# Attention and two gated MLPs on one core: the third stage of batch 1 placed before the first stage of batch 2

## The chip, the cores and the metric

The program runs on one core of a Trainium2 chip. The metric is device time in microseconds (us) of one execution. The core has a matrix engine (TensorE, PE in the profile), two elementwise engines (VectorE, DVE, and ScalarE, ACT), a general engine (GpSimd, POOL), and DMA engines that are fed by queues; nearly all transfers here are issued by SyncE (SP), some by POOL. Every engine works through its own list in order and waits on semaphores for the others.

## The reference

`q`, `k`, `v` have 4 batches, 12 heads, 448 rows and 64 columns, all float32. First attention, then two MLPs on the 1792 rows that it leaves:

```
q_n, k_n = rmsnorm(q, g_q), rmsnorm(k, g_k)
attn = softmax(q_n @ k_n.T / 8)            # per batch and head, 448 x 448
x = (attn @ v), heads side by side          # 1792 x 768
x = ((x @ w_a) * (x @ w_b)) @ w_out         # 768 -> 1536 -> 768
h = x @ w_in                                # 768 -> 2048
g = max(h, 0) + alpha * min(h, 0)
out = g @ w_out2                            # 2048 -> 768
```

## The kernel before

Products are made in float16 with a high and a low half of each number: a product of two tiles is three matmuls (high by high, high by low, low by high; `prod`). The kernel works batch by batch (448 rows), and the MLPs of a batch are four stages: **a** (`x @ w_a`, `x @ w_b` and their product, 24 units of 18 matmuls), **y** (times `w_out`, 12 units of 18), **h** (times `w_in`, then the activation, 16 units of 18) and **o** (times the last weight, 24 units of 12, then a transposition and the store). `a1` is stage a of batch 1, the second batch. The line `stages` lists the order. The stages `o2`, `y3` and `o3` use a product scheme with seven instead of eight block products; the weight sums for it are made by small steps in a list called `back`.

Attention runs ahead of the MLPs, in between their units. `att_steps` walks over 84 score tiles of two 128-row blocks each (21 for each batch). For one tile it issues the scores on PE (`scores`, 8 matmuls, tile `s`), the softmax on DVE and ACT (`soft`: L421 maximum, L434, L438 exponentials), the division and the split in halves (`probs`: L483 on ACT, L484 on DVE, tiles `p16`), DMA transposes into `pT`, and every three and a half tiles the product with v (`pv`, 24 matmuls into the one PSUM buffer `x`) and its split into the two halves of an `X` chunk (`pv_out`: L534 on ACT, L535 on DVE). Six chunks of 128 columns make the input of stage a of the next batch. `RATE` says how many of these tiles are issued during a stage, spread evenly over its units; before stage a of a batch, what is missing is issued at once.

Stage a ends with a scale that needs all 12 products: the product tiles are `ab32` (L1080 on DVE), ACT sums their squares (L1083), PE adds over the partitions (`tot`, into the same PSUM buffer as `pv`), DVE sums the columns (L135) and makes a power of two (`power`: L117, L120, L123), and ACT and DVE split the 12 tiles with it into halves `AB` (L894, L895). Where stage y of the same batch follows at once (`stages_after`), this is issued at once; otherwise it becomes a list of `tasks`, one for each following unit. Stage y splits each result with the same two lines into `Y` (also L894 and L895), stage h makes `G` (L1186, L1187, L1172, L1173).

Memory: `slot` has 35 buffers of 1792 bytes per partition for X, AB, Y and G. `raw` has 5 larger buffers, in which weights were converted earlier, and which the `back` steps use (one for what they load, one for sums). `BACK` says how many `back` steps are run with each unit of a stage that has no task.

The order on each engine is made from this program by a scheduler, which may move an instruction past others of its engine where nothing forbids it.

Of the kernel before, what the change touches and what calls it, by code (L numbers as in the profile page):

```python
# [9 lines left out]
F16 = mybir.dt.float16  # L10
BF16 = mybir.dt.bfloat16
I32 = mybir.dt.int32
I64 = mybir.dt.int64
# [6 lines left out]
def attention_gated_mlps_kernel(  # L20
# [16 lines left out]
    B, H, S, D = q.shape  # L37
# [11 lines left out]
    raw_p = ctx.enter_context(tc.tile_pool(name="raw", bufs=5))  # L49
# [17 lines left out]
    def slot(name):  # L67

        return slot_p.tile([128, 2, S], F16, tag="slot", name=name)
# [454 lines left out]
        d["x"] = ps  # L524

    X, Y, AB, G = {}, {}, {}, {}

    def pv_out(g):
        d = P[g]
        b, p = divmod(g, NP)  # L530
        ps = d["x"][:, 0:S]
        X[b, p] = x = slot(f"x{b}_{p}")
        s = sx[:, b:b + 1] if b == 0 else 2.0 ** -14
        nc.scalar.activation(out=x[:, 0], in_=ps, func=AF.Copy, scale=s)  # L534
        nc.vector.scalar_tensor_tensor(  # L535
            out=x[:, 1], in0=ps, scalar=s, in1=x[:, 0], op0=ALU.mult, op1=ALU.subtract
        )
        P[g] = None
# [5 lines left out]
    def att_steps():  # L544
# [3 lines left out]
        for m in range(total + 3):  # L548
# [41 lines left out]
            if done < B * NP and 2 * (m - 1) >= (done + 1) * NI:  # L590
                pv(done)
                pv_out(done)
                fin = done
                done += 1
            yield fin


    stages = "a0 y0 h0 o0 a1 y1 a2 h1 o1 y2 h2 a3 o2 y3 o2 h3 o3".split()
    FAST = ("o2", "y3", "o3")
    OPEN = "h2"  # L600
    PIECES = {"o2": [range(2), range(2, 3)]}
# [114 lines left out]
    for st in stages:  # L716
        n, parts, _ = CHAINS[st[0]]
# [536 lines left out]
            G.pop((b, f))  # L1254


    BACK = {"a2": 1, "o1": 1, "y2": 2, "a3": 3, "o2": 1, "y3": 1}
    RATE = {"a0": 4, "y0": 5, "h0": 4, "o0": 8, "a1": 14, "y1": 7, "a2": 4, "h1": 4, "o1": 8, "y2": 6}

    if True:  # L1260
        load_qk(0)
# [17 lines left out]
        n, done = 0, 0  # L1279
# [18 lines left out]
        for i, st in enumerate(stages):  # L1298
            s, b = st[0], int(st[1])
# [7 lines left out]
            if st == OPEN:  # L1307
# [9 lines left out]
                late["t"] = ctx.enter_context(tc.tile_pool(name="lt", bufs=4))  # L1317
            state["back"] = BACK.get(st, 0)
            n, parts, _ = CHAINS[s]
# [5 lines left out]
            else:  # L1325
                gen = gen[s](b)
            want, acc = 3 * RATE.get(st, 0), 0
            for _ in gen:
# [34 lines left out]
```

## Time and profile before

| | |
|---|---|
| median of 3 runs | 1214.35 us (1212.06 to 1216.56) |
| the profiled execution | 1215.08 us |
| its span, first to last instruction | 1213.0 us |
| PE busy | 1145.4 us, 94% of the span |
| DVE, ACT, POOL busy | 816.5, 770.1, 108.2 us |
| mean granted PE clock | 0.98 of full speed |
| HBM | 184 GB/s over the span |

In the rows below a stretch or a start is counted in us from the start of the span. Busy PE counts a matmul from its start to its end at whatever clock was granted, so a stretch in which PE is busy all the time can still be slow.

### The profile page before, as it was taken

How to read it: one execution, taken by the hardware profiler on the slowest of the kernel's cores; microseconds unless marked ns; L12 is line 12 of the kernel's file. 1: busy time of each engine (PE TensorE's matmuls, PEld its weight loads, DVE VectorE, ACT ScalarE, POOL GpSimd, SP SyncE). 2: the span in 40 equal slices, each digit the busy share in tenths (PEclk: the TensorE clock that was granted, in tenths of full speed). 3: DMA queues.
4: the chain of work that ended last, by engine and by line, in shares of the span. 5: the costliest groups of instructions: out<-in, count | busy, mean ns of one | idle time of the engine just before them, and what ended most of it. 6: DMA issues, size and time to landing. Idle time of an engine off the chain costs nothing. (4 is left out here: it accounts for less than half of the span.)

```text
span 1213.0 us, 20078 instructions
## 1 busy us (share of the span) xinstructions
PE 1145.4 (94%) x7144; PEld 650.6 (54%) x7144; DVE 816.5 (67%) x1695; ACT 770.1 (63%) x1543; POOL 108.2 (9%) x176
## 2 busy tenths in 40 slices
PE   6997999899989799998999999999999999999997
PEld 3553554445434344444445554544555558996597
DVE  7898999999899666677754376554356677523631
ACT  7998999999899666767534366564255335513532
POOL 1000000000001000000012100122200562000000
PEclk9997999999989899998999999999999999999999
DMA  7658999999999999987985677898834798873465
GB/s 190 174 163 211 315 326 329 288 298 305 309 246 308 252 237 253 248 199 173 198 225 152 159 175 164 199 222 190 228 117 135 247 299 284 272 210 107 129 188 171
DMA packets 319267, 269.78 MB, mean 222 GB/s; under 512 B 178464, under 2 KB 275232, under 8 KB 319168
## 3 DMA queue, kind: packets, MB, share of 16 engines
q1 hardware_dynamic: 311376, 246.41, 75.9%
q0 software_dynamic: 7792, 22.10, 6.3%
q8 instruction: 56, 0.92, 0.3%
q14 instruction: 43, 0.35, 0.1%
HBM read 179.77 MB, written 43.25 MB: 184 GB/s over the span
## 5 line engine op out<-in xcount | busy, mean ns | idle before, releaser
L110 PEld LDWEIGHTS <-w 128*128 128x128 f16 x4104 | 398.2, 99 | 393.5 <-issue 39.6
L110 PE MATMUL p<-x,w 128*128 128x448 f16 x1728 | 336.3, 354 | 0.5 <-DVE ab L1080 0.4
L110 PE MATMUL p<-y,w 128*128 128x448 f16 x1152 | 221.6, 352 | 1.4 <-DVE t L1187 1.3
L110 PEld LDWEIGHTS <-ws 128*128 128x128 f16 x1386 | 132.5, 98 | 3.3 <-DMA ws<-f_o_S 2.7
L110 PE MATMUL p<-ab,w 128*128 128x448 f16 x648 | 129.7, 359 | 1.3 <-ACT ab L894 1.2
L110 PE MATMUL p<-g,w 128*128 128x448 f16 x576 | 119.8, 362 | 4.6 <-ACT g L1172 3.5
L421 DVE TENSOR_REDUCE nm<-s 128x2 f32<-128x896 f32 x84 | 91.2, 1086 | 33.5 <-PE s L110 33.3
L483 ACT ACTIVATE p<-pf,ri 128x448 f16<-128x448 f32 x126 | 81.8, 665 | 35.9 <-DMA pT<-p 27.4
L484 DVE SCALAR_TENSOR_TENSOR p<-pf,ri,p 128x448 f16<-128x448 f32 x126 | 84.6, 680 | 28.1 <-ACT p L483 28.0
L110 PE MATMUL l<-g,ws 128*128 128x224 f16 x960 | 94.2, 259 | 1.8 <-DMA ws<-f_o_S 1.8
L438 ACT ACTIVATE pf<-s,nm,esc 128x448 f32<-128x448 f32 x126 | 90.0, 719 | 1.4
L832 DVE SCALAR_TENSOR_TENSOR w<-wf,sc,w 128x768 f16<-128x768 f32 (+1 forms) x76 | 70.1, 929 | 2.5 <-ACT w L831 2.1
L831 ACT ACTIVATE w<-wf,sc 128x768 f16<-128x768 f32 (+1 forms) x76 | 65.4, 869 | 2.6 <-DMA sc_h<-w 1.7
L764 ACT ACTIVATE wf<-raw 128x768 f32<-128x768 f32 (+1 forms) x76 | 63.6, 843 | 5.2 <-DMA raw<-in_moe_w_out_dram 3.2
L770 DVE SCALAR_TENSOR_TENSOR wf<-raw,wf 128x768 int32<-128x768 int32 (+1 forms) x76 | 65.7, 868 | 0.3
L1083 ACT ACTIVATE junk<-ab 128x448 bf16<-128x448 f32 x48 | 27.6, 574 | 59.8 <-DVE ab L1080 59.6
L778 ACT ACTIVATE junk<-wf 128x768 bf16<-128x768 f32 (+1 forms) x76 | 59.3, 781 | 1.3 <-DVE wf L770 1.3
L707 POOL DMA_DIRECT2D f_o_S<-raw x48 | 33.8, 807 | 292.6 <-DVE raw L703 214.0
L110 PE MATMUL s<-kT,qT 128*64 128x448 f16 x252 | 48.3, 375 | 11.6 <-DMA kT<-k 9.1
L1080 DVE SCALAR_TENSOR_TENSOR ab<-p,inv_a,t 128x448 f32<-128x448 f32 x48 | 32.5, 678 | 29.6 <-PE p L110 29.0
L110 PE MATMUL s<-early 128*128 128x448 f32 x84 | 39.6, 598 | 10.0 <-ACT pf L438 9.0
L110 PE MATMUL s<-kT,qS 128*64 128x448 f16 x252 | 46.7, 365 | 2.4 <-DMA qS<-qT 2.4
(171 smaller groups left out, 1434.1 us busy)
## 6 DMA issues: line engine op xcount, KB each, us to landing
w<-sc_a SPq DMA_DIRECT2D x72, 384.0 KB, 3.7
w<-sc_h SPq DMA_DIRECT2D x48, 384.0 KB, 3.1
raw<-in_moe_w_in_dram SPq DMA_DIRECT2D x16, 768.0 KB, 7.3
raw<-in_moe_w_out_dram SPq DMA_DIRECT2D x24, 512.0 KB, 6.1
ws<-f_o_S SPq DMA_DIRECT2D x48, 256.0 KB, 3.8
raw<-in_moe_w_a_dram SPq DMA_DIRECT2D x12, 768.0 KB, 7.3
raw<-in_moe_w_b_dram SPq DMA_DIRECT2D x12, 768.0 KB, 6.5
sc_a<-w SPq DMA_DIRECT2D x24, 384.0 KB, 7.3
```

The lines of the kernel that those rows point to most:

```text
L110: nc.tensor.matmul(out=o, lhsT=a, rhs=b, start=first, stop=last)
L421: nc.vector.tensor_reduce(out=nm, in_=ps[:, :, 0:S], axis=AX.X, op=ALU.max, negate=True)
L438: nc.scalar.activation(out=pf, in_=ps[:, j, 0:S], func=AF.Exp, bias=nm[:, j:j + 1], scale=scale[j], accum_out=su[:, j:j + 1],)
L483: nc.scalar.activation(out=t[:, 0, :, 0:KP], in_=pf, func=AF.Copy, scale=r)
L484: nc.vector.scalar_tensor_tensor(out=t[:, 1, :, 0:KP], in0=pf, scalar=r, in1=t[:, 0, :, 0:KP], op0=ALU.mult, op1=ALU.subtract,)
L707: nc.gpsimd.dma_start(out=formed[kind, i, name, j][:, :, cols], in_=d["x"][:, q])
L764: nc.scalar.activation(out=t, in_=hi.bitcast(F32), func=AF.Prelu, scale=2.0 ** -112, alpha=-(2.0 ** 32))
L770: nc.vector.scalar_tensor_tensor(out=ti, in0=lo, scalar=29, in1=ti, op0=ALU.logical_shift_right, op1=ALU.bitwise_or)
L778: nc.scalar.activation(out=junk(768, size(kind)), in_=t, func=AF.Square, accum_out=sums[0][:, j:j + 1])
L831: nc.scalar.activation(out=w[:, 0], in_=t, func=AF.Copy, scale=s)
L832: nc.vector.scalar_tensor_tensor(out=w[:, 1], in0=t, scalar=s, in1=w[:, 0], op0=ALU.mult, op1=ALU.subtract)
L1080: nc.vector.scalar_tensor_tensor(out=ab, in0=ps, scalar=i, in1=t, op0=ALU.mult, op1=ALU.mult)
```

## The change

There are four edits. In the order of stages, `h1` moves in front of `a2`. In `RATE`, the 42 score tiles of the last two batches are spread anew: a1, y1 and h1 get 10, 5 and 6 (before: a1 14, y1 7), and a2, o1 and y2 get 9, 7 and 5 (before: a2 4, h1 4, o1 8, y2 6). In `BACK`, o1 runs two steps with a unit instead of one; its first 14 units now carry the tasks of a2, which ran in h1 before. And the first three X chunks of the last batch lie in one `raw` buffer that is held until stage a3 has read them, so that `raw` has four buffers left meanwhile.

```diff
+    held, XR = [], 3
     def pv_out(g):
...
-        X[b, p] = x = slot(f"x{b}_{p}")
+        if b == B - 1 and p < XR:
+            if p == 0:
+                held.append(raw_p.tile([128, 784], I64, tag="raw", name="xraw").bitcast(F16)[:, 0:XR * 2 * S].rearrange("p (c l n) -> p c l n", c=XR, l=2))
+            x = held[0][:, p]
+        else:
+            x = slot(f"x{b}_{p}")
+        X[b, p] = x
...
-    stages = "a0 y0 h0 o0 a1 y1 a2 h1 o1 y2 h2 a3 o2 y3 o2 h3 o3".split()
+    stages = "a0 y0 h0 o0 a1 y1 h1 a2 o1 y2 h2 a3 o2 y3 o2 h3 o3".split()
...
-    BACK = {"a2": 1, "o1": 1, "y2": 2, "a3": 3, "o2": 1, "y3": 1}
-    RATE = {"a0": 4, "y0": 5, "h0": 4, "o0": 8, "a1": 14, "y1": 7, "a2": 4, "h1": 4, "o1": 8, "y2": 6}
+    BACK = {"a2": 1, "o1": 2, "y2": 2, "a3": 3, "o2": 1, "y3": 1}
+    RATE = {"a0": 4, "y0": 5, "h0": 4, "o0": 8, "a1": 10, "y1": 5, "h1": 6, "a2": 9, "o1": 7, "y2": 5}
```

In the changed file the lines behind the first edit are seven higher (L1080 becomes L1087, L894 becomes L901).

The first place is DVE's list at the end of a1, where the last product tile `ab32_1_11` and the scale `sab` of all twelve are made. Before:

```order
L476 TENSOR_SCALAR su_6476<-su_6476 128x2
L477 RECIPROCAL ri_6567<-su_6476 128x2
L535 SCALAR_TENSOR_TENSOR x2_3_6393<-x_6368,x2_3_6393 128x448
L390 SCALAR_TENSOR_TENSOR v16_6748<-vr_6109,sx_134,v16_6748 112x8x64
L484 SCALAR_TENSOR_TENSOR p16_0_111<-pf_6479,ri_6567,p16_0_111 128x4x112
L1080 SCALAR_TENSOR_TENSOR ab32_1_11_6417<-p_6396,inv_a_139,t_6340 128x448
L421 TENSOR_REDUCE nm_6559<-s_6466 128x2
L135 TENSOR_REDUCE tots_6423<-tot_6421 128x1
L484 SCALAR_TENSOR_TENSOR p16_1_112<-pf_6481,ri_6567,p16_1_112 128x4x112
L117 TENSOR_SCALAR pw_6425<-tots_6423 128x1
L421 TENSOR_REDUCE nm_6623<-s_6550 128x2
L120 TENSOR_SCALAR sab_136<-pw_6425 128x1
```

And now:

```order
L333 TENSOR_TENSOR qr_6630<-qr_6630,gbc_121 128x448
L476 TENSOR_SCALAR su_6275<-su_6275 128x2
L477 RECIPROCAL ri_6413<-su_6275 128x2
L484 SCALAR_TENSOR_TENSOR p16_0_111<-pf_6278,ri_6413,p16_0_111 128x4x112
L1087 SCALAR_TENSOR_TENSOR ab32_1_11_6216<-p_6195,inv_a_139,t_6170 128x448
L421 TENSOR_REDUCE nm_6405<-s_6265 128x2
L135 TENSOR_REDUCE tots_6222<-tot_6220 128x1
L421 TENSOR_REDUCE nm_6479<-s_6396 128x2
L117 TENSOR_SCALAR pw_6224<-tots_6222 128x1
L120 TENSOR_SCALAR sab_136<-pw_6224 128x1
```

The split of an X chunk (L535) and of v (L390) no longer stand ahead of the last product, and one of the two L484 between the product and the scale has moved behind it.

The second place is PE's list at the same seam, from `tot` (the sum over the partitions for the scale) on. `s` is a score tile, `x` a product with v, `w16` the weights of a unit. Before, a whole further score tile follows, and then the first matmul of y1:

```order
L110 MATMUL tot_6421<-ssab_133,ones_120 128x12
L110 LDWEIGHTS qT_6353
L110 MATMUL s_6614<-kT_6356,qT_6353 64x448
L110 LDWEIGHTS qT_6353
L110 MATMUL s_6614<-kT_6356,qT_6353 64x448
L110 LDWEIGHTS qS_6358
L110 MATMUL s_6614<-kT_6356,qS_6358 64x448
L110 LDWEIGHTS qS_6358
L110 MATMUL s_6614<-kT_6356,qS_6358 64x448
```

Now the rest of a score tile follows, and then the 24 matmuls of a `pv`, of which the first stand here:

```order
L110 MATMUL tot_6220<-ssab_133,ones_120 128x12
L110 LDWEIGHTS qT_6187
L110 MATMUL s_6396<-kT_6190,qT_6187 64x448
L110 LDWEIGHTS qS_6192
L110 MATMUL s_6396<-kT_6190,qS_6192 64x448
L110 LDWEIGHTS qS_6192
L110 MATMUL s_6396<-kT_6190,qS_6192 64x448
L110 LDWEIGHTS v16_5869
L110 MATMUL x_6348<-pT_5830,v16_5869 64x448
L110 LDWEIGHTS v16_5869
L110 MATMUL x_6348<-pT_5830,v16_5869 64x448
```

Ahead of `tot` stand two score tiles before (the list reaches the end of a1's last unit and then issues them) and one and five eighths now; the three of before have become two and a `pv`.

The third place is the new seam between y1 and h1. The last result of y1, `y1_5`, is split on ACT and then DVE; this is ACT's list around it now:

```order
L438 ACTIVATE pf_6782,su_6779<-s_6686,nm_6778,esc_125 128x448
L438 ACTIVATE pf_6784,su_6779<-s_6686,nm_6778,esc_125 128x448
L483 ACTIVATE p16_2_113<-pf_6782,ri_6938 128x4x112
L483 ACTIVATE p16_3_114<-pf_6784,ri_6938 128x4x112
L345 CAST q16_7334<-qr_6630 128x7x64
L347 CAST k16_7336<-kr_6631 112x8x64
L901 ACTIVATE y1_5_6766<-p_6685,cyf_130 128x448
L434 ACTIVATE nm_6903<-nm_6903,esc_125 128x2
```

On PE a score tile and the first 15 matmuls of h1 stand between the last matmul of y1 and the first reader of `y1_5`; before, a unit of a2 followed, which reads nothing that y1 makes.

## Rows read from the trace of the kernel before

**Rows 1.** Busy time by stretch: us, PE, PEld, DVE, ACT, POOL, clock, DMA, GB/s

```profile
437.90:549.50 111.60, 108.31 (x650) 52.03 (x648) 78.57 (x167) 75.92 (x175) 0.00 (x0) 0.98 1.01 231
553.30:605.20 51.90, 51.90 (x300) 25.45 (x299) 36.77 (x80) 32.13 (x68) 0.13 (x1) 0.96 0.77 182
694.00:756.00 62.00, 62.00 (x356) 30.99 (x354) 41.28 (x73) 39.43 (x78) 3.90 (x9) 1.00 0.76 171
```

**Rows 2.** Busy time of PE in stretches of 4 us: us, PE, clock, DMA, GB/s

```profile
436.00:440.00 4.00, 2.54 (x10) 0.74 0.97 279
...
548.00:552.00 4.00, 0.69 (x4) 0.82 0.95 248
552.00:556.00 4.00, 4.00 (x16) 0.50 0.88 200
556.00:560.00 4.00, 4.00 (x19) 0.83 0.17 44
```

**Rows 3.** Timeline at the end of a1: start, us, engine, line, instruction, idle before

```profile
544.55 0.38 PE L110 MATMUL s<-kT,qT 128*64 128x448 f16 x2
...
545.90 0.35 PE L110 MATMUL s<-kT,qS 128*64 128x448 f16 x2
...
547.49 0.68 DVE L484 SCALAR_TENSOR_TENSOR p<-pf,ri,p 128x448 f16<-128x448 f32 x1
548.09 0.68 DVE L1080 SCALAR_TENSOR_TENSOR ab<-p,inv_a,t 128x448 f32<-128x448 f32 x1
...
549.52 0.39 PE L110 MATMUL tot<-ssab,ones 128*128 128x12 f32 x2 [3.27 <-ACT junk L1083]
...
551.69 0.14 DVE L120 TENSOR_SCALAR sab<-pw 128x1 int32<-128x1 int32 x1
551.70 0.58 PE L110 MATMUL s<-kT,qT 128*64 128x448 f16 x2 [1.79 <-ACT pf L438]
...
552.01 6.80 ACT L894 ACTIVATE ab<-ab,sab 128x448 f16<-128x448 f32 x12
...
552.70 7.24 DVE L895 SCALAR_TENSOR_TENSOR ab<-ab,sab,ab 128x448 f16<-128x448 f32 x12 [0.52 <-ACT ab L894]
...
553.34 6.88 PE L110 MATMUL p<-ab,w 128*128 128x448 f16 x25
...
553.68 0.15 PEld L110 LDWEIGHTS <-w 128*128 128x128 f16 x1 [0.22 <-issue]
...
557.40 2.56 PEld L110 LDWEIGHTS <-w 128*128 128x128 f16 x14 [0.21 <-issue]
```

**Rows 4.** Timeline of PE within a1, undisturbed

```profile
463.29 2.46 PE L110 MATMUL x<-pT,v 112*64 112x448 f16 x24
465.68 3.58 PE L110 MATMUL p<-x,w 128*128 128x448 f16 x18
469.19 0.38 PE L110 MATMUL s<-kT,qT 128*64 128x448 f16 x2
```

**Rows 5.** Page, groups of the softmax: busy us, mean ns, idle before

```profile
L421 DVE TENSOR_REDUCE nm<-s 128x2 f32<-128x896 f32 x84 | 91.2, 1086 | 33.5 <-PE s L110 33.3
L483 ACT ACTIVATE p<-pf,ri 128x448 f16<-128x448 f32 x126 | 81.8, 665 | 35.9 <-DMA pT<-p 27.4
L484 DVE SCALAR_TENSOR_TENSOR p<-pf,ri,p 128x448 f16<-128x448 f32 x126 | 84.6, 680 | 28.1 <-ACT p L483 28.0
L438 ACT ACTIVATE pf<-s,nm,esc 128x448 f32<-128x448 f32 x126 | 90.0, 719 | 1.4
```

**Rows 6.** Timeline at the seam from y2 to h2

```profile
874.69 9.62 PE L110 MATMUL p<-y,w 128*128 128x448 f16 x50
874.89 0.63 ACT L894 ACTIVATE y<-p,cyf 128x448 f16<-128x448 f32 x1 [2.58 <-PE p L110]
875.56 0.68 DVE L895 SCALAR_TENSOR_TENSOR y<-p,cyf,y 128x448 f16<-128x448 f32 x1 [2.44 <-ACT y L894]
```

**Rows 7.** Timeline of PE within o0, its longest wait

```profile
398.67 0.58 PE L110 MATMUL s<-kT,qT 128*64 128x448 f16 x2 [5.44 <-DMA kT<-k]
```

## The prediction

> **What bounds the kernel now.** I read the page's shares first: PE is busy 94% of the span, no other engine above 67%. So only two things can shorten this kernel from an order of stages: time in which PE stands still, and time in which it runs at the lower of its two clocks (1.2 instead of 2.4 GHz). I then read the stretches by stage. From the start of a1 on PE is nearly always busy: 108.31 of 111.60 us in a1, 51.90 of 51.90 in the rest of y1, 62.00 of 62.00 in h1 [rows 1]. The reader is to see there that a1, with 14 score tiles, keeps DVE at 78.57 us (0.70 of the time) and ACT at 75.92 and still feeds PE. Next come the stretches of 4 us at the seam from a1 to y1, the one place in the changed region that stands out: PE works 0.69 of 4 us at 548 to 552, and then the granted clock is 0.50 for 4 us and 0.83 for the next [rows 2]. Last I read the timeline of that seam [rows 3].
>
> The last unit of a1 is done when the first score matmul behind it starts, at 544.55; I call this T. DVE gets to the last product tile only at T+3.54 (548.09), since the L484 at 547.49, which needs ACT, stands ahead of it, and ahead of that the splits of an X chunk and of v (the first list in the change). The sum `tot` starts 1.43 us later (549.52, after 3.27 us without work for PE). The scale is ready at 551.69, with another 1.79 us of standing still, the first ACT split starts at 552.01, and the first y1 matmul at 553.34. From there PE loads weights every 0.372 us (ten times from 553.68 to 557.40), which is half speed. Then it loads 14 in 2.56 us, full speed [rows 3].
>
> What is lost there, against undisturbed rows: a unit of 18 matmuls takes 3.51 us (465.68 to 469.19), so 0.195 each, and a `pv` 2.39 us (463.29 to 465.68) [rows 4]. A score tile takes 0.77 us: the two tiles from 544.55 have eight starts of pairs, the last at 545.90, 0.193 apart [rows 3]. From T to 557.40 pass 12.85 us. The work in it is three score tiles (2.31), `tot` (0.39) and eleven y1 matmuls (553.34 to 557.40 at 0.372 each; 2.15 at full speed): 4.85. So 8.0 us are lost: 5.06 standing still, 0.87 in the score tile at half speed (551.70 to 553.34 instead of 0.77), 1.9 in y1 at half speed, 0.2 between.
>
> The Trainium skill says that matmul busy time is a bad metric for the distance from full speed (Trainium Kernel Development and Optimization, Performance Expectations). By the busy time alone this seam would be worth 5.06 us; the spacing of the weight loads, which the trace has, makes it 8.0, and I use that.
>
> **The change part by part.** *Order of stages.* The matmuls of PE are the same in number and kind, so PE's work is unchanged; only seams change. The seam a1 to y1 stays, but the lists there differ.
>
> Now at T: DVE's list has the L484 of one tile directly ahead of the last product. Its scores stand two units ahead of T, that is 2 x 3.51, about 7.0 us. The chain from there is the maximum 1.09, two exponentials 1.44, L483 0.67, L484 0.68, together 3.9 us [rows 5], and four small steps between them, for which I put 1.0 (a handover with a small step took 0.32, 551.69 to 552.01 [rows 3]): 4.9. So DVE can be free at T at best, or up to 1.6 us late if the steps of the next q and k that stand in between hold it up; I take 0.5. Before it was 3.5.
> - From the product to `tot` 1.43 us (as before) plus 0.1 at the start: `tot` at T+1.55. PE has score work until T+1.16 (six of eight pairs), so 0.4 us idle.
> - `tot` ends at T+1.94, the rest of the score tile at T+2.3. Then `pv` needs the PSUM buffer, which DVE's column sum (L135) frees at about T+2.2. It runs 2.39 us: to T+4.7.
> - The scale: behind L135 stand one maximum (1.09) and three small steps: T+3.6. ACT has two exponentials meanwhile and starts the split at about T+3.9, as long after the scale as before (0.32); the first half tile is there at T+4.5, inside the `pv`. So the 1.79 us and the slow score tile are covered by the `pv`.
> - Then y1 eats a tile each 0.585 us (three matmuls) and DVE delivers one each 0.603 us (7.24 for 12) [rows 3]: 0.2 us over twelve tiles.
> Lost now: 0.4 + 0.1 (a first wait) + 0.2 + 0.5 (the late product) = 1.2 to 1.3 us, with the clock left at 2.4 GHz since PE never stands for more than about a microsecond. Gain 8.0 - 1.3 = 6.7 us. Bounds: 7.5 (nothing late), and 3.5 if the product is late by 1.6 and the clock falls as in the case below.
>
> *New seam y1 to h1.* h1 reads the last Y chunk as its sixth of six: one score tile (0.77) and 15 matmuls (2.93) are cover, 3.7 us. At the seam from y2 to h2 ACT starts 0.20 after the last y2 matmul and DVE ends the split 1.55 after it (876.24), and PE runs on without a wait [rows 6]. In the new list ACT has two exponentials, two L483 and two casts ahead of this split: the tile's scores end 7.0 us before the seam, the chain above up to L484 takes 4.9, the casts and their DVE steps some 1.3 (two at about L483's 0.67), so the split starts about 0.3 late and is over at about T'+2.0. I take 0; bounds 0 and 1.5, what is queued behind being h1's own evacuations. The cover that goes with the removed seam h1 to o1 cost nothing before either (62.00 of 62.00).
>
> *Spread.* One score tile costs DVE at most (78.57 - 12 x 0.68)/14 = 5.0 us. h1 gets two more tiles (+10.0) and loses the 12 splits of a2 (-8.2): 43 of some 65 us, 0.66, under a1's 0.70, at which PE did not wait [rows 1]. a2 and o1 come to about the same. I take 0, bounds -0.5 and +1.
>
> *`BACK` and the raw buffer.* o1 has 24 units, 14 with tasks, so 20 steps run in it; before 24. Up to a3 it is 24 + 20 + 24 = 68 instead of 72 of 144; the 4 left over run in the first units of o2, long before y3 needs them. With four buffers a block of sums still finds one: at most the block being stored, the one in use, its sums and the next one's load live together. 0; no row shows a raw buffer waited for by PE. Up to 1 us if a load comes late at the end of a3. X is read from the raw tile by the same matmuls; 0.
>
> Sum: 1215.08 (profiled) - 6.7 = 1208.4. The median of the runs shown is 0.73 lower than the profiled execution, so about 1207.7 for a median.
>
> **The rivals.** *The clock falls all the same.* At 436 to 440 PE was busy 2.54 of 4 us, far from empty, and the granted clock was 0.74 [rows 2]. The new seam has `tot`, waits of tenths and the late product in about 5 us. If it falls there, y1 starts with about eleven matmuls at half speed (1.9 us), and with the product late by 1.5 the gain is 8.0 - 1.3 - 1.9 - 1.1 = 3.7: 1210.7. Against it: the stretch before this clock was emptier at the old seam (0.69 of 4). The skill has a rule that speaks for this rival: micro-idles of PE between groups of matmuls can make the clock swing, even with no long gap (TensorE: Matmul & The Clock Gate, A second HAM failure mode). No row here shows short idles alone doing it; by the rule the time would be this rival's.
>
> *The seam stays as it was* (DVE again 3 us late): 1214, since the new place of the `pv` behind `tot` would still give back 1 us or so at most.
>
> *The transposes come late at a new seam: slower.* `pT`, `q16` and `k16` have one buffer each, and all transposes stand in SP's list behind weight loads and behind each other. In o0 PE stood 5.44 us for a kT [rows 7]. If at y1 to h1 the casts ahead of the last Y split wait like that, the split is 5.4 late where the cover leaves 1.7 (3.7 less 2.0): 3.7 of standing still and, as at the old seam, 0.9 + 1.9 at half speed, 6.5 in all, which eats the gain: 1214. If the scores of h1, which now has six tiles, wait for kT at its two changes of chunk as well, 5.44 + 2.8 twice more, 1207.7 + 6.5 + 16.5 = 1231; one such wait more, 1222. It decides from where a transpose lands over 1.7 us late. Against it: a1 had 14 tiles in 111.6 us, y1 7 in 51.9, both denser than any stage now (6 in 65), and PE did not wait for a transpose there [rows 1].
>
> **How the numbers follow.** Within 0.5%, about 6.1 us, a measurement can hardly tell this kernel from no change: 1208.3 to 1220.4. The forecast (1205.5 to 1210, its middle 1207.7) has 0.68, some 0.72 of it below 1208.3. The fallen clock (about 1209 to 1212.5) has 0.15, the unchanged seam 0.07, late transposes 0.10, 0.07 of that past 1220.4. Faster by over 0.5%: 0.68 x 0.72 = 0.49. Slower: 0.07. Same: the rest, 0.44. The range from 1204.5 to 1214.5 holds the forecast, the fallen clock and the unchanged seam, and leaves out the late transposes.
>
> **What would show it.** Right: in the stretch after the last unit of a1 the last L1087 starts within about a microsecond of T, `tot` is preceded by under 1 us of idle time, a `pv` runs between `tot` and y1, weight loads of y1 start 0.19 apart at once, and no 4 us stretch there has a clock under 0.9. The first h1 matmuls follow y1 without a gap. Wrong: a clock of 0.5 behind the seam, an L1087 three microseconds late, or a wait of PE in h1, a2 or o1 that rows before do not have, on a DMA above all.

## The result: slower, 1232 us instead of 1215

Six runs of each on the same chip: 1232.17 us (1226.50 to 1236.83) against 1214.59 us (1210.35 to 1219.56) for the kernel before. The ratio is 1.0141, 95% interval 1.0105 to 1.0176. The forecast was 1207.7 and the range ended at 1214.5, so both missed. The profiled execution took 1230.12 us, span 1228.0.

PE has 1148.2 us of busy time, 2.8 more than before. The time was lost by standing still and by a low clock. These are the six stages that the change touches, in the stretches view of the changed kernel (us from start to end, length, busy PE, PEld, DVE, ACT, POOL, clock, DMA, GB/s; in order a1, y1, h1, a2, o1, y2, each from its first matmul to the first of the next):

```profile
435.56:548.02 112.46, 105.57 (x592) 51.19 (x591) 67.86 (x149) 63.62 (x147) 1.08 (x4) 0.94 0.83 199
548.02:595.91 47.89, 47.89 (x277) 23.60 (x276) 25.52 (x46) 25.87 (x53) 0.00 (x0) 1.00 0.75 174
595.91:664.37 68.46, 65.91 (x389) 32.62 (x387) 47.11 (x95) 40.51 (x84) 0.00 (x0) 1.00 0.70 175
664.37:762.38 98.01, 94.86 (x546) 47.00 (x545) 55.69 (x109) 50.05 (x114) 16.17 (x24) 1.00 0.89 204
762.38:839.72 77.34, 71.69 (x427) 36.05 (x426) 44.47 (x86) 44.69 (x90) 13.56 (x23) 0.99 0.80 180
839.72:887.28 47.56, 47.56 (x273) 24.00 (x273) 18.32 (x33) 12.92 (x26) 13.67 (x21) 0.98 0.78 227
```

Together 451.7 us. In before the same stages took 436.7 (a1 115.4, y1 51.9, a2 88.7, h1 62.0, o1 71.8, y2 46.8), for the same matmuls: 15.0 more, which is the whole difference of the spans (1228.0 - 1213.0). Where [rows 1] had busy PE equal to the stretch in y1 and h1, a1 now lacks 6.9 us, h1 2.6, a2 3.2 and o1 5.7. y1 is as dense as before.

`RATE` tells in which stage a tile is issued, and the scheduler then moves some. What PE ran in each stage by the trace, and what the stage lost or gained beyond it (a tile at 0.77 us and a `pv` at 2.39, as in the prediction):

| stage | before: us, tiles, `pv` | changed: us, tiles, `pv` | beyond the tiles, us |
|---|---|---|---|
| a1 and y1 | 167.3, 20, 6 | 160.4, 15, 4 | +1.7 |
| h1 | 62.0, 5, 1 | 68.5, 6, 2 | +3.3 |
| a2 | 88.7, 4, 1 | 98.0, 8, 2 | +3.8 |
| o1 | 71.8, 8, 2 | 77.3, 8, 2 | +5.5 |
| y2 | 46.8, 1, 2 | 47.6, 1, 2 | +0.7 |

So no stage gained, and o1 has as many tiles as it had before.

**The seam a1 to y1** is where the gain was forecast. Timeline from the last unit's end, T = 536.95 (start, us, engine, line, instruction, idle before):

```profile
529.38 0.63 ACT L236 ACTIVATE sk<-kr 112x512 f32<-112x512 f32 x1 [1.71 <-DMA kr<-in_k_dram]
...
530.05 0.69 DVE L240 TENSOR_REDUCE stat<-sk 112x8 f32<-112x512 f32 x1 [2.17 <-ACT sk L236]
...
536.95 0.38 PE L110 MATMUL s<-kT,qT 128*64 128x448 f16 x2
536.98 1.08 DVE L421 TENSOR_REDUCE nm<-s 128x2 f32<-128x896 f32 x1
...
538.42 0.72 ACT L438 ACTIVATE pf<-s,nm,esc 128x448 f32<-128x448 f32 x1
...
539.84 0.63 ACT L1084 ACTIVATE t<-p,inv_a 128x448 f32<-128x448 f32 x1
...
540.00 0.38 PE L110 MATMUL s<-kT,qT 128*64 128x448 f16 x2 [2.10 <-ACT pf L438]
...
541.74 0.68 DVE L1087 SCALAR_TENSOR_TENSOR ab<-p,inv_a,t 128x448 f32<-128x448 f32 x1
...
543.17 0.60 PE L110 MATMUL tot<-ssab,ones 128*128 128x12 f32 x2 [2.44 <-ACT junk L1090]
...
548.02 0.36 PE L110 MATMUL p<-ab,w 128*128 128x448 f16 x1
```

The last product is at T+4.79 (before T+3.54 [rows 3], forecast T+0.5), and PE stands twice. The `pv` does fill the wait for the scale, as forecast, but at half clock: the stretches of 4 us here, beside those of [rows 2]:

```profile
536.00:540.00 4.00, 1.90 (x15) 0.77 (x14) 3.75 (x7) 2.54 (x8) 0.00 (x0) 1.00 0.48 125
540.00:544.00 4.00, 1.56 (x9) 0.98 (x10) 2.77 (x6) 2.29 (x6) 0.00 (x0) 0.60 0.69 148
544.00:548.00 4.00, 4.00 (x24) 1.78 (x20) 2.84 (x9) 3.23 (x8) 1.08 (x4) 0.54 0.01 2
```

So why was DVE late? The first two rows of the timeline tell one part: ACT's square of the next k (`sk`, L236) waited 1.71 us for the load of `kr`, and DVE waited 2.17 us for the square before its sum L240. Behind that sum stand the small steps of the next q and k up to 535.85, then an old product, and only then the maximum of the tile, at 536.98. ACT's exponentials come behind the maximum, and the last L1084 behind them.

The wait is less than half of it. The product comes 4.3 us later than forecast, and the wait accounts for 2.2 of them at most. The rest is the work behind the sum, which holds DVE from 530.05 to 536.98 (0.64 us of it a wait for the square of q, 0.68 the old product). The runs below in which the same steps stand there point the same way: where the square waited only 1.17 us (e10) the product still came at T+3.71, and where it waited 4.77 (e6) at T+5.57. In e5, where no square waits for a load at the seam, the sums and the small steps still stand on DVE from T-3.78 on, and the product comes at T+4.80.

**Inside a1** PE stood once more, and there it was the square of the next q (`sq`, L239) that waited for its load. SP, ACT and PE:

```profile
490.94 0.57 SPq L210 DMA_DIRECT2D qr<-in_q_dram  x1
...
495.04 0.58 ACT L239 ACTIVATE sq<-qr 128x448 f32<-128x448 f32 x1 [2.42 <-DMA qr<-in_q_dram]
...
499.08 5.25 PE L110 MATMUL p<-x,w 128*128 128x448 f16 x18 [2.35 <-ACT t L1084]
```

In ACT's list the L1084 that PE waits for stands behind this square, with the softmax of one tile between them.

**The same in a2**, in full size (SP's issue of the load, then ACT, DVE and PE):

```profile
678.39 0.42 SPq L206 DMA_DIRECT2D kr<-in_k_dram  x1
...
684.95 0.63 ACT L236 ACTIVATE sk<-kr 112x512 f32<-112x512 f32 x1 [8.01 <-DMA kr<-in_k_dram]
...
685.61 0.69 DVE L240 TENSOR_REDUCE stat<-sk 112x8 f32<-112x512 f32 x1 [8.04 <-ACT sk L236]
...
688.47 0.68 DVE L1087 SCALAR_TENSOR_TENSOR ab<-p,inv_a,t 128x448 f32<-128x448 f32 x1
...
689.20 1.10 PE L110 MATMUL p<-x,w 128*128 128x448 f16 x5 [2.37 <-DVE ab L1087]
```

The load lands 6.5 us after its issue. Meanwhile ACT and DVE both stand, though PE has finished results for them. Here are 4 us of h1 and 4 us of a2:

```profile
604.00:608.00 4.00, 3.91 (x25) 1.83 (x23) 0.00 (x0) 0.00 (x0) 0.00 (x0) 1.00 0.87 275
...
680.00:684.00 4.00, 4.00 (x23) 2.08 (x22) 0.00 (x0) 0.00 (x0) 0.00 (x0) 1.00 1.12 263
```

The third and fourth of the busy columns, DVE and ACT, are zero. PE works on as long as it has a free buffer for its products, and then stands for an instruction of DVE: 2.11 us in h1 (up to 610.02) and 2.37 in a2 (up to 689.20). The Trainium skill says that the queues of ScalarE and VectorE are strictly first in, first out (TensorE: Matmul & The Clock Gate, Architectural detail: the array is 16× 32×32, not 1× 128×128); these two rows agree.

In all, the view of waits has (engine, line, what it waited for, us, times, longest) for the changed kernel

```profile
ACT sk L236 <- DMA kr<-in_k_dram: 31.0, 8, 8.0
```

and for before 19.4 us, 8 times, longest 5.7. Behind that longest one, in a2, PE stood for only 0.42 us, where the 8.0 cost 2.37. The runs that come below have the same three places with other waits (us the square waited, then us PE stood behind it; blank where that square had no such wait):

| place | changed | e3 | e6 | e9 | e11 | e10 |
|---|---|---|---|---|---|---|
| h1, square of k | 5.52, 2.11 | 4.51, 1.10 | 5.32, 1.91 | | 5.62, 2.21 | |
| a2, square of k | 8.01, 2.37 | 6.61, 0.63 | 7.11, 1.88 | 7.79, 2.08 | 10.27, 4.51 | |
| a1, square of q | 2.42, 2.35 | 2.44, 2.69 | | | 2.82, 3.01 | 4.52, 4.56 |

In h1 PE stands for the wait less 3.41 us in all four, so what PE has in its buffers covers 3.4 us there; in a2 it covers between 5.2 and 6.0, in a1 next to nothing. Where e1, e9 or e10 take the wait away, the idle time there is gone.

**o1** has another reason. At its end (ACT and PE):

```profile
834.91 0.67 ACT L483 ACTIVATE p<-pf,ri 128x448 f16<-128x448 f32 x1 [0.85 <-ACT pf L438]
835.48 1.12 ACT L709 CAST raw<-raw 128x512 f16<-128x512 f32 x2
836.51 0.67 ACT L483 ACTIVATE p<-pf,ri 128x448 f16<-128x448 f32 x1
837.08 1.04 ACT L1211 ACTIVATE t<-p,inv_o 128x448 f32<-128x448 f32 x1
838.18 1.10 PE L1222 MATMUL p<-ident,t 128*112 128x128 f32 x4 [2.83 <-ACT t L1211]
```

The evacuation of o1 (L1211) stands behind the softmax and behind two `back` casts (L709) of one unit.

### The profile page after: what moved, and what is told of

It reads as the page before. It is cut to its first block, busy times and chain, and to the rows that moved or that the text cites. A ratio compares the mean times of both kernels' runs of the same rounds, so it can differ in the third digit from the quotient of the medians.

```text
span 1228.0 us, 20066 instructions
## 1 busy us (share of the span) xinstructions
PE 1148.2 (94%) x7144; PEld 651.5 (53%) x7144; DVE 818.6 (67%) x1695; ACT 768.7 (63%) x1543; POOL 107.5 (9%) x176
## 5 line engine op out<-in xcount | busy, mean ns | idle before, releaser
L110 PE MATMUL p<-x,w 128*128 128x448 f16 x1512 | 300.6, 355 | 5.5 <-ACT t L1084 3.1
L484 DVE SCALAR_TENSOR_TENSOR p<-pf,ri,p 128x448 f16<-128x448 f32 x126 | 84.3, 682 | 40.6 <-ACT p L483 40.5
L110 PE MATMUL x<-pT,v 112*64 112x448 f16 x432 | 48.4, 375 | 1.0 <-DVE tots L135 0.9
```

The source lines that it names most:

```text
L110: nc.tensor.matmul(out=o, lhsT=a, rhs=b, start=first, stop=last)
L484: nc.vector.scalar_tensor_tensor(out=t[:, 1, :, 0:KP], in0=pf, scalar=r, in1=t[:, 0, :, 0:KP], op0=ALU.mult, op1=ALU.subtract,)
```

## The experiments

The theory (A in the expectations): a square that the list puts close behind the load of its k, and a load that lands late, stop ACT and, through the sum, DVE. Rivals: the new spread is too dense (B); the k come too late for the scores themselves (C); the two `back` steps a unit in o1 (D, for o1 only). All ratios are to the kernel before on the same chip; the changed kernel has 1.0141. "Stages" is a1 to y2 in the profiled execution, "wait" is L236 for `kr` over the whole run, without the waits for `qr`.

| run | us | ratio (95%) | stages us | wait us |
|---|---|---|---|---|
| before | | 1 | 436.7 | 19.4 |
| changed | 1232.17 | 1.0141 (1.0105 to 1.0176) | 451.7 | 31.0 |
| e1 squares pinned | 1210.48 | 0.9964 (0.9941 to 0.9988) | 435.5 | 4.9 |
| e2 old density | 1237.08 | 1.0187 (1.0153 to 1.0221) | 446.3 | 19.2 |
| e3 `back` one in o1 | 1230.64 | 1.0133 (1.0093 to 1.0174) | 444.6 | 27.5 |
| e4 squares on POOL | 1225.41 | 1.0103 (1.0067 to 1.0138) | 454.7 | (DVE) 32.9 |
| e5 before, pinned | 1211.50 | 0.9971 (0.9950 to 0.9993) | 438.6 | 4.4 |
| e6 loads on POOL | 1238.44 | 1.0207 (1.0180 to 1.0233) | 457.1 | 36.0 |
| e7 pinned, steps in h2 | 1205.15 | 0.9938 (0.9915 to 0.9962) | 428.9 | 4.6 |
| e8 pinned, steps in y2 | 1213.08 | 0.9996 (0.9978 to 1.0015) | 436.1 | 4.5 |
| e9 pairs 12 to 19 pinned | 1217.91 | 1.0051 (1.0029 to 1.0072) | 443.6 | 16.9 |
| e10 pairs 20 to 23 pinned | 1219.51 | 1.0046 (1.0024 to 1.0069) | 448.7 | 7.3 |
| e11 steps in h2 alone | 1225.67 | 1.0089 (1.0065 to 1.0113) | 451.8 | 31.7 |

**e1.** The one line that keeps the squares where the program has them:

```diff
-    PIN0, PIN1 = (1, 2, 3), ()
+    PIN0, PIN1 = (1, 2, 3), tuple(range(12, 24))
```

> The changed kernel with one line different: for the last two batches the ACT square of a new k (L236) keeps its place in program order, so it no longer stands directly behind the time at which the scheduler thinks the k has landed, but later and next to the square of the following pair. Theory A (ACT's list in order: a square that waits for a late k holds up exponentials and evacuations behind it, and PE runs out of buffers): the waits of L236 for the DMA of kr fall from 31 us to under 12 us, the idle times of PE at 499, 540, in h1 at 610 and in a2 at 689 (2.35, 2.10, 2.11, 2.37 us) vanish or halve, the half clock at the end of a1 with them; 7 to 12 us less than the changed kernel, 1220 to 1225 where that is 1232. Theory B (density: ten tiles in a1, six in h1 and nine in a2 at these places make ACT and DVE late whatever the loads do): within 3 us of the changed kernel. Theory C (the k and q themselves arrive too late for the scores): PE waits for kT or qT instead, no gain. The loss in o1 stays in all of them.

Measured: 1.77 points less than the changed kernel, some 21 us, about twice what was expected, and a little less than before. The waits are gone, and with them every idle time of PE over 0.5 us from a1 to a2 (a1 102.3 us, y1 47.9, h1 66.3, a2 94.6); o1 keeps its loss. The transfers are as long as they were; this one was issued at 590.98 and took

```profile
DMA to landing us min/median/max: 7.6/7.6/7.6
```

but its square stands 48 us further on in ACT's list and waits for nothing:

```profile
638.71 0.61 ACT L236 ACTIVATE sk<-kr 112x512 f32<-112x512 f32 x1
```

That refutes B and C for these stages: same tiles in the same stages, loads as long, and no PE wait for a kT or qT. But the one line moves more than the wait. The square of q, the sums and the small steps all come behind the square of k, and they move with it: in e1 none of these stands on DVE between 16 us ahead of T and 6 us behind it. So at the seam e1 takes the wait and the work away together. And the seam is now what the prediction said it would be, with T = 532.40:

```profile
532.40 0.38 PE L110 MATMUL s<-kT,qT 128*64 128x448 f16 x2
532.58 0.69 DVE L1087 SCALAR_TENSOR_TENSOR ab<-p,inv_a,t 128x448 f32<-128x448 f32 x1 [0.18 <-PE p L110]
...
534.02 0.39 PE L110 MATMUL tot<-ssab,ones 128*128 128x12 f32 x2
...
534.67 2.24 PE L110 MATMUL x<-pT,v 112*64 112x448 f16 x21
...
536.32 4.02 ACT L901 ACTIVATE ab<-ab,sab 128x448 f16<-128x448 f32 x7
...
537.03 0.35 PE L110 MATMUL p<-ab,w 128*128 128x448 f16 x1
```

Product at T+0.18 (forecast T+0.5), `tot` at T+1.62 (T+1.55), the first split at T+3.92 (T+3.9), the clock 1.00 in each stretch of 4 us from 522 to 542. From T to the first matmul of y1 pass 4.63 us, in which two tiles (1.54), `tot` (0.39) and a `pv` (2.39) are 4.3 of work: 0.3 lost where before had lost 8.0. So the seam gave 7.7, forecast 6.7. Over a1 and y1 together, 150.3 us instead of 167.3 with 8.6 us of tiles and `pv` fewer, the gain is 8.4.

**e9 and e10** pin one part of the squares each (`range(12, 20)`, `range(20, 24)`).

> The changed kernel with the squares L236 kept in program order for the pairs 12 to 19 alone; those are the squares that in the changed kernel stand up to the end of a1 (the last of them at 529.38). The four squares after it stay where they were. If the waits of e1 act each at its own place, a1 loses its standing still and its half clock (112.46 to about 102.3), h1 (68.5) and a2 (98.0) keep theirs: 8 to 11 us less than the changed kernel. If any change of the list helps as a whole, by chance, the stages change otherwise.

> The other half: pairs 20 to 23 alone, whose squares in the changed kernel waited at 569, 608, 635 and 685. a1 stays at about 112.5 with its seam, h1 goes from 68.5 to about 66.4 and a2 from 98.0 to about 94.6: 4 to 7 us less than the changed kernel. e9 and e10 together should give about what e1 gave.

Measured: e9 a1 103.8 us, a2 99.5, h1 66.5 (it should have kept 68.5: the list moved one of the late squares as well). e10 a1 115.1 (its q waited 4.52 us there instead of 2.42), h1 65.9, a2 94.6. Each repairs its own stages, and the other keeps its loss. The ratios are 0.90 and 0.95 points under the changed kernel, together 1.85, where e1 has 1.77. The 0.95 of e10 is more than the 4 to 7 us expected; its stages in the profiled execution, 3.0 us less, don't account for it all.

**e4 and e6** leave the squares where they are and take away one side of the wait.

```diff
-        i = nc.scalar.activation(out=sk, in_=d["kr"], func=AF.Square)
+            nc.gpsimd.tensor_tensor(sk, d["kr"], d["kr"], op=ALU.mult)
...
-        nc.sync.dma_start(
+        (nc.gpsimd if g >= 2 * NP else nc.sync).dma_start(
```

(The first pair is e4, with the same for q; the second e6, for k and q.)

> The changed kernel with the squares of k and q of the last two batches on POOL instead of ACT (two multiplications of a tile with itself for each pair), so that no ACT instruction waits for a load of k or q. POOL has some 108 us of work in 1228. The sums of the squares stay on DVE. Theory A: as e1 or a little better, 1218 to 1225, if the DVE sums do not wait for POOL in the place of ACT; where they do (L242 waiting for sk over 1.5 us, with an L421 behind it), half of the gain is lost. Theory B and C: within 3 us of the changed kernel, 1229 to 1235.

> The changed kernel, not pinned, with the loads of k and q of the last two batches issued by POOL instead of SP, so that they no longer stand behind transposes and weight loads in SP's list. It tells why the k is late. If the place in SP's list makes it late (issued at 523.94, where its buffer was free earlier), the loads start earlier, the waits of L236 for kr fall from 31 us under 15 us and the time to 1213 to 1223. If the transfer itself is slow in a burst of loads (5.4 to 7.2 us from issue to landing), or the buffer comes free only then, the waits stay near 31 us and the time within 3 us of the changed kernel, 1229 to 1235.

e4 gained 4.6 us by the ratios, with intervals that overlap, and not in these stages (454.7 us against 451.7): its a1 begins 5.4 us earlier. The wait only changed its engine; the waits of DVE have

```profile
DVE stat L242 <- POOL sk L237: 32.9, 10, 7.2
```

(L242 is the sum, L237 the square, in e4's lines.) e6 lost 8 us. POOL waits for nothing but the buffer, and issues the load as soon as DVE (L356) has read the last of the old k:

```profile
519.25 0.69 DVE L356 TENSOR_TENSOR k<-kr,k 112x512 f16<-112x512 f32 x1 [0.43 <-ACT k L347]
520.24 0.68 POOL L206 DMA_DIRECT2D kr<-in_k_dram  x1 [0.55 <-DVE k L356]
527.60 0.63 ACT L236 ACTIVATE sk<-kr 112x512 f32<-112x512 f32 x1 [4.77 <-DMA kr<-in_k_dram]
```

Its landing takes 7.3 us all the same, and the waits came to 36.0 us. So SP's list is not what makes these k late: in the changed kernel the last seven loads of k were issued at most 1.8 us after their buffer was free. The buffer comes free late and the transfer is long, longer still from POOL (median of the last twelve loads of k 6.1 us against 4.2). The Trainium skill says that spreading transfers over the issuing engines gives no bandwidth, since all use the same DMA engines (DMA: Bandwidth & Descriptors, Rules for kernel authors); these landings, which did not get shorter, agree. A third buffer for k would be the direct test; it was not tried.

For the q that stopped a1 it was SP's list: DVE had read the last of the old q at 479.00, and the load was issued 11.9 us later, behind transposes and other loads. In e6 it is issued 0.3 us after its buffer is free, and its wait is gone, but the square of the k beside it now waits 6.12 us.

**e5**, the same one line in the kernel before:

> The kernel before, with the squares L236 of the last two batches kept in program order and nothing else. In before these squares waited 19.4 us for kr, but PE stood still for it only some 0.6 us in the stages from a1 on. Theory A as it now stands (the wait costs where PE has no buffered work beside it, which the changed order brings about): within 3 us of before, 1210 to 1214. If pinning is simply a better list for any order, so that the change itself gave nothing, before gains as much as e1 showed against it or more: 1207 to 1210, and the old seam from a1 to y1 (5.06 us of standing still) would have to be shorter.

It gained 3.5 us, but not at the seam, where the squares with their sums and small steps came to stand and PE stood 4.53 + 1.79 us (before 3.27 + 1.79), and not in the stages (438.6). Its a1 only begins earlier (432.16 instead of 437.98). Why the stages ahead of a1 are shorter is not settled; the start of a1 lies between 430.0 and 442.2 in the profiles here, pinned or not.

**e2**, the old density in the new order:

```diff
-"a1": 10, "y1": 5, "h1": 6, "a2": 9, "o1": 7, "y2": 5}
+"a1": 14, "y1": 7, "a2": 7, "o1": 8, "y2": 6}
```

> The changed order of stages with the spread of before as far as it can be had: a1 14, y1 7, h1 none (before: 14, 7), then 7, 8 and 6 in a2, o1 and y2 (before a2 4, h1 4, o1 8, y2 6); o1 takes one BACK step a unit as before, and a3 four instead of three. Beside the run with o1 at one step and the new spread (e3) only the spread differs. If the loss comes from the new spread, this one is at or under the kernel before: 1205 to 1215, with the gain at the seam a1 to y1 lost again, since the old list stands there. If the swap itself costs (splits of a2 as tasks in o1, the new seams), it stays 6 to 10 us above before. Theory A expects no fixed number here, but that every idle time of PE over 1 us, wherever it lies, has an L236 or L239 that waits for kr or qr over 1.5 us within 8 us ahead of it.

It is the slowest but one, so the old spread does not bring the time back. Its seam is the old one (2.22 and 1.79 us of standing still), but a1, y1 and h1 together, with 21 tiles by `RATE` as in e3, took 219.8 us against 227.8 in e3; a2, o1 and y2, 21 tiles by `RATE` in both, 226.4 against 216.8. The loss lies in o1, 80.7 us against 73.0, and in y2, 51.1 against 46.8. In o1 PE waits here:

```profile
768.82 4.02 ACT L901 ACTIVATE ab<-ab,sab 128x448 f16<-128x448 f32 x7 [1.09 <-DVE sab L120]
772.75 1.05 ACT L1211 ACTIVATE t<-p,inv_o 128x448 f32<-128x448 f32 x1
...
773.85 1.10 PE L1222 MATMUL p<-ident,t 128*112 128x128 f32 x4 [4.59 <-ACT nm L434]
```

The evacuation (L1211) stands behind seven of the twelve splits of a2 (L901). That is not enough for a cause: e3 has seven splits in a row too, 4.01 us, and both run eight tiles in o1 by the trace. In e2 ACT had also waited 3.29 us for a transpose of q just ahead. What makes this o1 so much longer is open. My expectation that each long idle time has a late square just ahead of it fails here: these have splits ahead of them. Both e2 and e3 also lost 8.4 and 7.5 us in o2 (36.4 in the changed kernel) with their fourth step in a3.

**e3, e7, e8, e11**: where the `back` steps go.

```diff
-    BACK = {"a2": 1, "o1": 2, "y2": 2, "a3": 3, "o2": 1, "y3": 1}
+    BACK = {"a2": 1, "o1": 1, "y2": 2, "a3": 4, "o2": 1, "y3": 1}            (e3)
+    BACK = {"a2": 1, "o1": 1, "y2": 2, "h2": 1, "a3": 3, "o2": 1, "y3": 1}   (e7, e11)
+    BACK = {"a2": 1, "o1": 1, "y2": 3, "a3": 3, "o2": 1, "y3": 1}            (e8)
```

> The changed kernel with one BACK step a unit in o1, as before, and four instead of three in a3, so that the weights are ready in time. Theory D (the forming of weights in o1, two steps a unit on ACT and DVE beside seven tiles and the splits of a2, makes o1 late): o1 takes 3 to 6 us less (77.3 in the changed kernel, 71.8 before), a3 at most 1 us more: 1226 to 1230 where the changed kernel has 1232. If the transposes of p alone hold up ACT there, or the splits, o1 changes by under 1.5 us and the time by nothing.

> e1 with one BACK step a unit in o1 instead of two, and one in h2, which has none otherwise (no attention runs there), instead of the fourth in a3 that cost e3 7.5 us in o2. If theory D holds and h2 has room, o1 takes 3 to 4.5 us less than in e1 (76.3), o2 stays at 36: 1206 to 1208, under both kernels. If the steps are late again for the weights of o2, o2 takes up to 7 us more and the time is that of e1 or more, 1210 to 1214.

> e1 with one BACK step a unit in o1 and three instead of two in y2, beside five score tiles. If the steps cost where ACT and DVE carry softmax as well, y2 (48.0 in e1) takes 1 to 3 us more and o1 3 to 4.5 less: 1207 to 1210. If only o1 is tight, because of the splits of a2 ahead of the steps, y2 stays: 1206 to 1208.

> The changed kernel, not pinned, with the BACK steps of e7 (one a unit in o1 and in h2). It has the waits of the squares, so only the steps' share shows: o1 from 77.3 to about 73, y2 from 47.6 to 46.9, 4 to 6 us less than the changed kernel, 1226 to 1228. If the gain of e7 over e1 came from something else than o1 and y2 (a1 was 1.8 us shorter too), less than 3 us.

D holds for o1 in all four: 73.0, 72.9, 73.0 and 72.9 us, against 77.3 (76.3 in e1). The steps that were taken out have to fit elsewhere. In e3 the last product of a3 comes behind them, and PE waits early in o2, so that the time is that of the changed kernel:

```profile
1032.16 0.60 PE L110 MATMUL p<-ssab,ones 128*128 128x12 f32 x2 [6.32 <-ACT junk L1090]
```

In e8 y2 grew to 54.1 us, by one wait for a weight that the expectation did not foresee:

```profile
857.79 4.43 PE L110 MATMUL p<-ab,w 128*128 128x448 f16 x13 [5.25 <-DMA w<-sc_y]
```

SP had issued loads of these weights at 850.48, behind three transposes of `p` that held its list for 9.9 us; whether the steps brought that about is open. In h2, without softmax, the steps cost nothing (54.5 us as in the changed kernel). e11, not pinned, gained 0.52 points; in its profiled execution a late square of 10.3 us in a2 takes the 4.4 of o1 back. e7 is the best of all, 0.6% under before. Its a1, h1 and o1:

```profile
432.36:532.89 100.53, 100.30 (x594) 50.06 (x591) 58.42 (x125) 59.93 (x139) 0.45 (x3) 1.00 0.91 220
...
580.82:646.88 66.06, 65.67 (x388) 32.49 (x387) 45.39 (x91) 41.83 (x84) 0.00 (x0) 1.00 0.70 181
...
741.48:814.41 72.93, 71.03 (x428) 35.76 (x426) 37.82 (x72) 41.97 (x83) 8.35 (x16) 1.00 0.77 177
```

Its stages are 7.8 us shorter than before. Against e5, the pinned kernel before, the ratios differ by 0.33 points with intervals of about 0.2 on each side, so that this last comparison is at the edge of what the runs resolve.

## Why the prediction was wrong

**The step that failed** is the one on DVE at T: "So DVE can be free at T at best, or up to 1.6 us late if the steps of the next q and k that stand in between hold it up; I take 0.5." DVE was 4.8 us late. I had put those steps at no more than 1.6 us of work. Their head, the sum L240, also waits for a load that lands 5.4 us after its issue, which cost DVE 2.17 us; and the work behind it is long: it ends, with the old product, only when T has come, and then the maximum of the tile is still to be made. So the work was sized too small, and the wait was left out. How the 4.3 us over the forecast divide between the two is not shown exactly; the work without a wait, in the other list of e5, made the product 4.80 us late. From T to the first matmul of y1 pass 11.07 us with 4.3 of work, so 6.7 are lost, half clock included, and of the 8.0 us at the seam 1.3 came back instead of 6.7. e1, without wait and work, has 0.3 lost.

**Spread ("I take 0, bounds -0.5 and +1")** failed mostly by waits. The shares of DVE were near what I put (47.1 of 68.5 us in h1, 0.69). But a share says nothing of a list in order: with DVE at 0.69, four whole microseconds of h1 had no work on it. Beyond their tiles h1 took 3.3 us more and a2 3.8; e1 gives back 2.1 and 3.4 of these, and another 3.7 in a1 ahead of T.

**`BACK` (put at 0)** failed: two steps a unit in o1, behind the splits of a2, cost 4.4 us there. I had weighed only whether the steps would be done in time and not what they stand ahead of on ACT. With the splits, o1 took 5.5 us more, at the same eight tiles.

Sum: a1 and y1 were to gain 6.7 us and lost 1.7, 8.4 missed; h1, a2, o1 and y2 lost 3.3, 3.8, 5.5 and 0.7. That makes 21.7, by which the forecast of the span was missed (15.0 + 6.7).

**What held.** The seam's mechanism, to a few tenths, in e1. The new seam y1 to h1: 0.44 us of idle time, inside the bounds of 0 and 1.5. The raw buffer: h2 took 54.5 us and a3 81.7, before and after. PE's work: the same matmuls. The counts of tiles per stage did not hold: the prediction took them from `RATE`, and a1 of before had 16 by the trace.

**The rivals.** "The clock falls all the same" happened (0.60 and 0.54), but behind a product 4.8 us late; in e1, with the product in time and 0.3 us lost in all, it stayed at 1.00, so whether it holds through the microsecond that the forecast allowed was not put to the test. "The transposes come late" had the right form, a transfer that lands late and stops an engine's list, and named its slower side; that one of its times, 1231, is near the measured one is chance. The wrong transfer was looked at: it was loads of k and q and not transposes. What I put against it, that denser stages did not wait before, was no evidence: in a1 of before, the densest of them, the squares had waited 1.1, 1.1 and 2.6 us without PE running dry. The rows of waits with 19.4 us for `kr` were in the trace of before and were not weighed.

## What to carry to other kernels

Where a scheduler sets the order of an engine's list, look in the trace of before for instructions that wait long for a load and happen to cost nothing: any change that moves tiles can turn them into standing time, and one that keeps such an instruction, and the work that hangs on it, far behind its load (here one line, 21 us) can be worth more than a better seam. A busy share of 0.7 says nothing on whether an engine is there when it is needed; ask what its list holds ahead of the instruction that counts, and when the last input of that lands. Test a lost gain by removing the wait and keeping the change, and pin part by part, to see that each stage gets back its own loss; then look what else the pin has moved, as here the steps behind the square.

## What was not expected of the hardware

One load of k (112 x 512 float32) took from 2.5 to 7.7 us from issue to landing in the changed kernel, median 3.5; those of 5.4 and more had loads of weights close to them in SP's list, but so had one of 3.2. What sets the length of one transfer was not measured by itself.

Standing still of nearly the same length had different results for the clock. After 2.35 us in a1 the next stretch of 4 us was granted 0.59; after 2.37 us in a2 it stayed at 1.00:

```profile
496.00:500.00 4.00, 1.66 (x13) 0.82 (x10) 1.66 (x5) 3.10 (x7) 0.00 (x0) 0.98 0.63 237
500.00:504.00 4.00, 4.00 (x15) 1.66 (x12) 2.00 (x4) 2.90 (x8) 0.00 (x0) 0.59 0.00 0
...
688.00:692.00 4.00, 2.80 (x15) 1.46 (x15) 3.79 (x10) 2.58 (x6) 1.40 (x2) 1.00 0.40 137
692.00:696.00 4.00, 4.00 (x23) 1.96 (x20) 3.76 (x12) 0.00 (x0) 0.00 (x0) 1.00 0.33 104
```

What tells the two apart is open.
